# A gated recurrence and a top-2 router: TensorE's order written out by hand, one activation table, accumulating scatters, two weight buffers

## The chip, the cores and the metric

The kernel runs on one core of a Trainium2 chip. The metric is the device time of one execution in microseconds (us). The engines are TensorE (PE; its weight loads are listed as PEld), VectorE (DVE), ScalarE (ACT), GpSimd (POOL) and SyncE (SP), which here only issues DMAs.

## The reference

There are two parts, all in float32. The first is a gated recurrence for 4 batches of 8 heads, 768 steps, and a head size of 48; the second is a mixture of 8 experts over the 3072 rows of 384 numbers which the first part gives.

```python
f = 1 / (1 + exp(-f_logit))
for t in range(768):                              # per batch and head
    state = f[t][:, None] * state + outer(k[t], v[t])
    y[t] = q[t] @ state
x = y as rows: (batch, step) by (head, dim)       # 3072 x 384
noisy = x @ w_gate + log1p(exp(x @ w_noise)) * noise
top2 of 8 experts per row; their weights are a softmax over the two
out[row] = sum over its two experts e: weight * (relu(x[row] @ w1[e]) @ w2[e])
# w1[e] is 384 x 1024, w2[e] is 1024 x 384
```

## The kernel before

**Attention.** The steps are cut into 6 chunks of 128 per batch: 24 chunks, numbered n = c * 4 + b. All 8 heads of a chunk are one tile of 128 x 512 (each head padded to 64 columns). Five stages handle a chunk:

- `forget` (L480): POOL clamps f; PE transposes it; ACT makes exp, then ln(1 + .); POOL writes the first column of `cap` (L489); VectorE's scan adds up along the chunk (L490); ACT makes P = exp(-L) and Q = exp(L).
- `scaled` (L498): PE transposes q and k; VectorE multiplies them by P and Q (qP, kQ).
- `scores` (L504): PE multiplies kQ by qP; VectorE masks the result (A); PE transposes kQ back and ACT copies it (kn).
- `output` (L520): y is the sum of v by A (L526, 128 rows of the array) and of state by qP (L530, 64 rows), which alternate by pairs of heads; ACT copies it. Then ds = kn by v gives the next state of the batch (L539 to L549).
- `features` (L552): PE transposes y, ACT copies it and SP writes it to `x_rows` in DRAM; PE makes the router's logits (L563) in a PSUM bank that the four batches of a chunk share.

After each fourth chunk `route` (L567) makes the two experts of each of 512 rows, counts rows per expert with the matmuls L604 and L605 (`rk`), and POOL scatters one entry of 4 words for each row and expert into `lists` (L627): 8 indirect DMAs, 48 in all. An entry holds the row to read, the row of `out` to add (or a far one if this is the row's first expert), the weight, and the row of `out` to write.

**FFN.** `plan` (L634) forms 55 tiles of up to 128 rows, each of one expert, and writes to `steer` for each tile its expert, its place in the lists and whether its weights have to be loaded. For a tile, `fetch` (L671) has SP load the list entries and POOL gather the rows (L679); `weights` (L683) loads w1 and w2 (1.5 MB each) into one of NR = 3 buffers if `new` is set; `turned` (L688) transposes the rows; `hidden` (L696) makes 8 blocks of 128 hidden units with 48 matmul instructions, and ACT applies ReLU after each half (L704); `result` (L707) clears `had` and gathers the rows of `out` written so far into it (L710), multiplies by w2 (L715), scales and adds on VectorE (L718) and scatters to `out` (L720). `out` is zeroed at the start by 24 DMAs on POOL (L736).

**What sets the order.** The stages are written as a software pipeline (L741 to L749) and a loop over tiles (L764 to L772). A scheduler of the framework then orders the instructions of each engine by their place in the program and by modelled times of readiness, so an engine's order is not the written one. Each engine and each DMA queue works in its own order. PSUM has 4 single banks (`one_bank`) and 2 double ones (`two_banks`); a tile gets a bank when its last user is done. Dependencies of PSUM tiles are tracked by tile: in `hidden` the second half waits for ACT's read of the first.

Of the kernel before, what the change touches and what calls it, by code (L numbers as in the profile page):

```python
# [329 lines left out]
def kernel(  # L330
# [30 lines left out]

# [12 lines left out]
    NR = 3  # L374
# [24 lines left out]
    NLD = 4  # L399
    PAD = {"f": 30.0, "q": 0.0, "k": 0.0, "v": 0.0}  # L400
    pads = {n: [const.tile([C, H, DP], F32, tag=f"{n}{i}", name=f"{n}{i}") for i in range(NLD)] for n in "fqkv"}
    for i in range(NLD):
        for n in "fqkv":
            nc.vector.memset(pads[n][i][:, :, D:DP], PAD[n])

# [26 lines left out]
    for i, val in enumerate((0, FAR, 0, FAR)):  # L432
        nc.vector.memset(empty[:, :, i], val)
# [3 lines left out]
    for i in range(2):  # L437
        nc.gpsimd.memset(cap[i], LCAP)

# [27 lines left out]
    def load(n):  # L467
        c, b = n // B, n % B
        for nm, src in (("f", f_logit), ("q", q), ("k", k), ("v", v)):
            nc.sync.dma_start(out=pads[nm][n % NLD][:, :, 0:D],  # L470
                              in_=src[b, :, c * C:(c + 1) * C, :].rearrange("h t d -> t h d"))

    def transposed(nm, n):
        p = one_bank(f"{nm}p_{n}")
        flat = pads[nm][n % NLD].rearrange("t h d -> t (h d)")
        for hp in range(HP):
            nc.tensor.transpose(p[:, cols(hp)], flat[:, cols(hp)], ident)  # L477
        return p

    def forget(n):  # L480
        raw = pads["f"][n % NLD].rearrange("t h d -> t (h d)")
        nc.gpsimd.tensor_scalar(raw, raw, XMIN, None, ALU.max)  # L482
# [37 lines left out]
    def output(n):  # L520
        c, b = n // B, n % B
        vt = pads["v"][n % NLD]
# [29 lines left out]
    def features(n):  # L552
# [9 lines left out]
        for hp in range(HP):  # L562
            nc.tensor.matmul(lg[c][:, b, :], lhsT=yT[n][:, cols(hp)], rhs=w_rt[:, hp, :],  # L563
                             start=(hp == 0), stop=(hp == HP - 1))


    def route(c):  # L567
# [40 lines left out]
        late = t([B, 2], "late")  # L608
        nc.vector.tensor_tensor(late[:, :, 0:1], fx[:, :, 0:1], fx[:, :, 1:2], ALU.is_gt)
        nc.vector.tensor_tensor(late[:, :, 1:2], fx[:, :, 1:2], fx[:, :, 0:1], ALU.is_gt)  # L610
        entry = t([B, 2, 4], "entry", U32)
        tok = token[:, c, :].unsqueeze(2).broadcast_to((128, B, 2))
        prev = t([B, 2], "prev")
        nc.vector.tensor_scalar(prev, tok, -float(FAR), None, ALU.add)
        nc.vector.tensor_tensor(prev, prev, late, ALU.mult)
        nc.vector.tensor_scalar(entry[:, :, :, 1], prev, float(FAR), None, ALU.add)
        nc.vector.tensor_copy(entry[:, :, :, 0], tok)
        nc.vector.tensor_copy(entry[:, :, :, 3], tok)
        nc.vector.tensor_copy(entry[:, :, :, 2].bitcast(F32), ex)
# [5 lines left out]
        for b in range(B):  # L625
            for r in range(2):
                put = nc.gpsimd.indirect_dma_start(  # L627
                    out=lists, out_offset=bass.IndirectOffsetOnAxis(ap=sloti[:, r, b:b + 1], axis=0),
                    in_=entry[:, b, r, :], in_offset=None)
# [39 lines left out]
    w2 = [const.tile([128, FO, DM], F32, tag=f"w2_{i}", name=f"w2_{i}") for i in range(NR)]  # L669

    def fetch(t, steer):  # L671

        slots = ffn.tile([128, 4], U32, tag="slots", name=f"slots{t}", bufs=6)
        e, row, new = (nc.values_load(steer[0:1, t, i:i + 1], engines=[mybir.EngineType.SP], min_val=0, max_val=hi,
                                      skip_runtime_bounds_check_because="clamped where they are made")
                       for i, hi in ((0, E - 1), (1, E * N), (2, 1)))
        nc.sync.dma_start(out=slots, in_=lists[bass.ds(row, 128), :])
        xg = ffn.tile([128, DM], F32, tag="xg", name=f"xg{t}", bufs=4)
        nc.gpsimd.indirect_dma_start(out=xg, out_offset=None, in_=x_rows,  # L679
                                     in_offset=bass.IndirectOffsetOnAxis(ap=slots[:, 0:1], axis=0))  # L680
        return slots, xg, e, new

    def weights(t, e, new):  # L683
        i = t % NR
        nc.sync.dma_start(out=w1[i], in_=moe_w1[bass.ds(e, 1)].rearrange("o (k p) f -> p (o k) f", p=128), cond=new)
        nc.sync.dma_start(out=w2[i], in_=moe_w2[bass.ds(e, 1)].rearrange("o (f p) d -> p (o f) d", p=128), cond=new)

    def turned(t, xg):  # L688
        xp = one_bank(f"xgp{t}")
        for i in range(KO):  # L690
            nc.tensor.transpose(xp[:, i * 128:(i + 1) * 128], xg[:, i * 128:(i + 1) * 128], ident)  # L691
        xt = ffn.tile([128, KO, 128], F32, tag="xt", name=f"xt{t}")
        nc.vector.tensor_copy(xt, xp[:, 0:DM].rearrange("d (k t) -> d k t", k=KO))  # L693
        return xt

    def hidden(t, xt):  # L696
        hp = two_banks(f"hp{t}").rearrange("f a (o t) -> f a o t", t=128)
        hs = ffn.tile([128, FO, 128], F32, tag="hs", name=f"hs{t}")
        for fo in range(FO):
            for i in range(KO):  # L700
                nc.tensor.matmul(hp[:, fo // 4, fo % 4, :], lhsT=w1[t % NR][:, i, fo * 128:(fo + 1) * 128],  # L701
                                 rhs=xt[:, i, :], start=(i == 0), stop=(i == KO - 1))
# [4 lines left out]
    def result(t, hs, slots):  # L707
        had = ffn.tile([128, DM], F32, tag="had", name=f"had{t}")
        nc.gpsimd.memset(had, 0.0)  # L709
        nc.gpsimd.indirect_dma_start(out=had, out_offset=None, in_=out,  # L710
                                     in_offset=bass.IndirectOffsetOnAxis(ap=slots[:, 1:2], axis=0),
                                     bounds_check=N - 1, oob_is_err=False)
        yp = one_bank(f"yp{t}")
        for fo in range(FO):
# [3 lines left out]
        nc.vector.scalar_tensor_tensor(ys, in0=yp[:, 0:DM], scalar=slots[:, 2:3].bitcast(F32), in1=had,  # L718
                                       op0=ALU.mult, op1=ALU.add)
        nc.gpsimd.indirect_dma_start(out=out, out_offset=bass.IndirectOffsetOnAxis(ap=slots[:, 3:4], axis=0),  # L720
                                     in_=ys, in_offset=None, bounds_check=N - 1, oob_is_err=False)
# [17 lines left out]
    for n in range(NLD):  # L739
        load(n)  # L740
    for i in range(-2, NS + 2):  # L741
        for stage, lag in ((forget, -2), (scaled, -1), (scores, 0), (output, 1), (features, 2)):
            n = i - lag
            if 0 <= n < NS:
                stage(n)
                if stage is output and n + NLD < NS:
# [58 lines left out]
```

## Time and profile before

| what | value |
|---|---|
| median of 3 runs | 1020.29 us (1019.8 to 1022.79) |
| profiled execution | 1024.36 us, span 1022.6 us |
| mean granted clock of TensorE | 0.911 |
| PE busy | 859.0 us (84%) |
| weight loads busy | 673.4 us (66%) |
| VectorE, ACT, POOL busy | 194.5, 237.2, 312.3 us |
| DMA | 130.6 MB in 159,887 packets, mean 128 GB/s |

The span runs from the first to the last instruction. A share of busy time is a mean over two stages with different limits, so it says little by itself. The granted clock is the share of full speed (2.4 GHz) that TensorE got; 0.5 is its lower level, 1.2 GHz. Rows of matmuls have modelled ends and overlap, so starts are used for times between them. Where a row ends in square brackets, the engine sat idle before it for that many us, and the name is what ended this.

### The profile page before, as it was taken

The numbers are of one execution on the slowest core, as the hardware profiler recorded it, in microseconds if no ns is written. First come the engines' busy times: TensorE is split into PE (matmuls) and PEld (weight loads), VectorE is DVE, ScalarE is ACT, GpSimd is POOL, SyncE is SP. The second block draws the span as 40 slices with busy tenths as digits, with TensorE's granted clock in tenths as the row PEclk, the third lists the DMA queues.
The fourth block names the chain that finished last, engine by engine and source line by source line (L and its number), as shares of the span: only waits on it lengthen the run. The fifth ranks groups of instructions, "written<-read, shape, count | busy, mean of one in ns | idle before, by whom it ended". The sixth has DMA issues, their size and how long they took to land. (4 is left out here: it accounts for less than half of the span.)

```text
span 1022.6 us, 14847 instructions
## 1 busy us (share of the span) xinstructions
PE 859.0 (84%) x5777; PEld 673.4 (66%) x5777; DVE 194.5 (19%) x519; ACT 237.2 (23%) x357; POOL 312.3 (31%) x406
## 2 busy tenths in 40 slices
PE   0687979697891678899999899899899899999995
PEld 0575657475661556677777777677677677777773
DVE  1454434434503000000100010011010000011000
ACT  0785666565611000000101001001001001001010
POOL 7623343423033122232332333232223223233321
PEclk9898787887855889999999999899999999999998
DMA  9963525351100906616615713731841842941100
GB/s 297 116 121 72 102 59 100 66 106 33 39 24 17 383 25 217 217 42 214 230 37 165 268 51 109 248 119 49 284 159 49 283 165 63 315 138 55 47 18 4
DMA packets 159887, 130.60 MB, mean 128 GB/s; under 512 B 115045, under 2 KB 143353, under 8 KB 159808
## 3 DMA queue, kind: packets, MB, share of 16 engines
q1 hardware_dynamic: 145920, 99.61, 34.3%
q0 software_dynamic: 13888, 29.94, 9.3%
q8 instruction: 48, 0.79, 0.3%
q14 instruction: 31, 0.25, 0.1%
HBM read 213.75 MB, written 20.74 MB: 229 GB/s over the span
## 5 line engine op out<-in xcount | busy, mean ns | idle before, releaser
L701 PEld LDWEIGHTS hp<-xt,w 128*128 128x128 f32 x2640 | 315.6, 196 | 47.7 <-ACT hs L704 32.3
L701 PE MATMUL hp<-xt,w 128*128 128x128 f32 x2640 | 325.4, 281 | 22.5 <-ACT hs L704 21.8
L715 PE MATMUL yp<-w,hs 128*128 128x384 f32 x880 | 294.8, 489 | 0.0
L715 PEld LDWEIGHTS yp<-w,hs 128*128 128x128 f32 x880 | 164.2, 192 | 103.0 <-issue 1.8
L704 ACT ACTIVATE hs<-hp 128x512 f32<-128x512 f32 x110 | 65.7, 597 | 628.7 <-PE hp L701 613.3
L720 POOL DMA_INDIRECT out_dram<-ys,slots x55 | 55.2, 1004 | 290.0 <-DVE ys L718 289.7
L718 DVE SCALAR_TENSOR_TENSOR ys<-yp,slots,had 128x384 f32<-128x384 f32 x55 | 34.0, 618 | 439.6 <-PE yp L715 330.5
L710 POOL DMA_INDIRECT had<-out_dram,slots x55 | 56.6, 1030 | 179.1 <-issue 138.5
L691 PE MATMUL xgp<-ident,xg 128*128 128x128 f32 x165 | 29.3, 288 | 50.4 <-DMA xg<-x_rows,slots 50.3
L693 DVE COPY xt<-xgp 128x384 f32<-128x384 f32 x55 | 30.7, 558 | 187.3 <-PE xgp L691 181.5
L679 POOL DMA_INDIRECT xg<-x_rows,slots x55 | 53.0, 964 | 30.4 <-issue 14.3
L627 POOL DMA_INDIRECT lists<-entry,sloti x48 | 46.8, 975 | 32.2 <-DVE sloti L624 17.1
L691 PEld LDWEIGHTS xgp<-ident,xg 128*128 128x128 f32 x165 | 19.9, 146 | 53.2 <-issue 33.1
L526 PE MATMUL y<-A,v 128*64 128x128 f32 x384 | 47.5, 333 | 5.1 <-issue 4.8
L482 POOL TENSOR_SCALAR f<-f 128x512 f32<-128x512 f32 x24 | 36.6, 1527 | 31.4 <-DMA f<-in_f_logit_dram 31.3
L477 PE MATMUL fp<-ident,f 128*128 128x128 f32 x96 | 20.7, 355 | 29.2 <-POOL f L482 29.2
L530 PE MATMUL y<-qP,st 64*64 64x128 f32 x320 | 42.0, 343 | 1.7 <-issue 1.7
L490 DVE TENSOR_TENSOR_SCAN L<-f,cap 128x512 f32<-128x512 f32 x24 | 30.0, 1255 | 48.4 <-POOL cap L489 47.6
L526 PEld LDWEIGHTS y<-A,v 128*64 128x64 f32 x384 | 21.9, 153 | 23.0 <-issue 22.1
L477 PEld LDWEIGHTS fp<-ident,f 128*128 128x128 f32 x96 | 16.4, 205 | 29.6 <-POOL f L482 29.6
L530 PEld LDWEIGHTS y<-qP,st 64*64 64x64 f32 x320 | 18.6, 154 | 21.0 <-issue 21.0
L508 PE MATMUL sc<-qP,kQ 64*128 64x128 f32 x384 | 31.9, 312 | 0.0
(120 smaller groups left out, 621.1 us busy)
## 6 DMA issues: line engine op xcount, KB each, us to landing
w<-in_moe_w_dram SPq DMA_DIRECT2D x110, 1536.0 KB
f<-in_f_logit_dram SPq DMA_DIRECT2D x24, 192.0 KB
q<-in_q_dram SPq DMA_DIRECT2D x24, 192.0 KB
k<-in_k_dram SPq DMA_DIRECT2D x24, 192.0 KB
v<-in_v_dram SPq DMA_DIRECT2D x24, 192.0 KB
out_dram<-zero POOLq DMA_DIRECT2D x24, 192.0 KB
x_rows<-xs SPq DMA_DIRECT2D x24, 192.0 KB
slots<-lists SPq DMA_DIRECT2D x55, 2.0 KB
```

The source lines that it names most:

```text
L477: nc.tensor.transpose(p[:, cols(hp)], flat[:, cols(hp)], ident)
L482: nc.gpsimd.tensor_scalar(raw, raw, XMIN, None, ALU.max)
L526: nc.tensor.matmul(y[rows(par), cols(hp)], lhsT=vt[:, 2 * hp + par, :], rhs=A[n][:, par, cols(hp)], start=True, stop=(c == 0))
L530: nc.tensor.matmul(y[rows(par), cols(hp)], lhsT=state[b][rows(par), hp, :], rhs=qP[n][rows(par), cols(hp)], start=False, stop=True)
L627: put = nc.gpsimd.indirect_dma_start(out=lists, out_offset=bass.IndirectOffsetOnAxis(ap=sloti[:, r, b:b + 1], axis=0), in_=entry[:, b, r, ...
L679: nc.gpsimd.indirect_dma_start(out=xg, out_offset=None, in_=x_rows, in_offset=bass.IndirectOffsetOnAxis(ap=slots[:, 0:1], axis=0))
L691: nc.tensor.transpose(xp[:, i * 128:(i + 1) * 128], xg[:, i * 128:(i + 1) * 128], ident)
L701: nc.tensor.matmul(hp[:, fo // 4, fo % 4, :], lhsT=w1[t % NR][:, i, fo * 128:(fo + 1) * 128], rhs=xt[:, i, :], start=(i == 0), stop=(i == ...
L704: nc.scalar.activation(hs[:, fo - 3:fo + 1, :], hp[:, fo // 4], AF.Relu)
L710: nc.gpsimd.indirect_dma_start(out=had, out_offset=None, in_=out, in_offset=bass.IndirectOffsetOnAxis(ap=slots[:, 1:2], axis=0), bounds_ch ...
L715: nc.tensor.matmul(yp[:, 0:DM], lhsT=hs[:, fo, :], rhs=w2[t % NR][:, fo, :], start=(fo == 0), stop=(fo == FO - 1))
L720: nc.gpsimd.indirect_dma_start(out=out, out_offset=bass.IndirectOffsetOnAxis(ap=slots[:, 3:4], axis=0), in_=ys, in_offset=None, bounds_che ...
```

## The change

- **Order.** `in_order` adds to each TensorE instruction a scheduling edge from the one written before it, from the first load on. The other engines are ordered as before.
- **State matmuls.** In `output` all 8 pairs of v by A come first, then all of state by qP, with one start flag per bank.
- **Tables.** One set of ACT's tables, which has exp and ln, is loaded at the start.
- **Loads.** f, q and k have 3 buffers and v has 4. Each is refilled right behind the stage that last reads it, and the clamp of f moves from `forget` to the load.
- **Zeros.** The 24 writes of zeros to `out` move from POOL to SP, one behind each `output`.
- **Router.** The logits of a chunk get a bank of their own and are copied by ACT. `route` is cut in two: the part from `rk` on is written one iteration later. The row numbers of all entries are made at the start.
- **Scatters.** An entry holds the row, the weight, and the row of `out`. POOL's scatter adds to `out` in DRAM; `had`, its clearing and its gather go.
- **FFN.** NR is 2. List entries are loaded 4 tiles ahead and rows gathered 3 ahead, both written ahead of `hidden`; w1 of tile t + 2 is asked for behind `hidden(t)`, w2 behind `result(t)`. `turned(t + 1)` is written between `hidden(t)` and `result(t)`, as before.

```diff
-    NR = 3
+    NR = 2
...
-    NLD = 4
+    RING = {"f": 3, "q": 3, "k": 3, "v": 4}
...
+    nc.scalar.preload_act_table_set("natural_log_exp_and_others")
...
+    entry = const.tile([128, NCH, B, 2, 4], U32, tag="entry", name="entry")
+    nc.vector.memset(entry, 0)
+    for i in (0, 2):
+        nc.vector.tensor_copy(entry[:, :, :, :, i], token.unsqueeze(3).broadcast_to((128, NCH, B, 2)))
...
-    def load(n):
+    def load(nm, n):
         c, b = n // B, n % B
...
+        if n < NCH * B:
+            nc.sync.dma_start(out=pads[nm][n % RING[nm]][:, :, 0:D],
...
+            if nm == "f":
+                raw = pads["f"][n % RING["f"]].rearrange("t h d -> t (h d)")
+                nc.gpsimd.tensor_scalar(raw, raw, XMIN, None, ALU.max)
...
         for hp in range(HP):
             for par in range(2):
                 nc.tensor.matmul(y[rows(par), cols(hp)], lhsT=vt[:, 2 * hp + par, :], rhs=A[n][:, par, cols(hp)],
-                                 start=True, stop=(c == 0))
-            if c:
+                                 start=(hp == 0), stop=(c == 0 and hp == HP - 1))
+        if c:
+            for hp in range(HP):
                 for par in range(2):
                     nc.tensor.matmul(y[rows(par), cols(hp)], lhsT=state[b][rows(par), hp, :],
-                                     rhs=qP[n][rows(par), cols(hp)], start=False, stop=True)
+                                     rhs=qP[n][rows(par), cols(hp)], start=False, stop=(hp == HP - 1))
...
+        lp = one_bank(f"lp_{n}")[:, 0:2 * E]
+        for hp in range(HP):
+            nc.tensor.matmul(lp, lhsT=yT[n][:, cols(hp)], rhs=w_rt[:, hp, :],
+                             start=(hp == 0), stop=(hp == HP - 1))
         if b == 0:
-            lg[c] = one_bank(f"lg_{c}")[:, 0:B * 2 * E].rearrange("t (b e) -> t b e", b=B)
...
+            lg[c] = rt.tile([128, B, 2 * E], F32, tag="lg", name=f"lg_{c}")
+        nc.scalar.copy(lg[c][:, b, :], lp)
...
+        yield
         rk = one_bank(f"rk_{c}")[:, 0:B * E].rearrange("t (b e) -> t b e", b=B)
...
-        late = t([B, 2], "late")
...
+        nc.vector.tensor_copy(entry[:, c, :, :, 1].bitcast(F32), ex)
...
-    def result(t, hs, slots):
-        had = ffn.tile([128, DM], F32, tag="had", name=f"had{t}")
-        nc.gpsimd.memset(had, 0.0)
-        nc.gpsimd.indirect_dma_start(out=had, out_offset=None, in_=out,
...
+        nc.vector.tensor_scalar(ys, yp[:, 0:DM], slots[t][:, 1:2].bitcast(F32), None, ALU.mult)
+        nc.gpsimd.indirect_dma_start(out=out, out_offset=bass.IndirectOffsetOnAxis(ap=slots[t][:, 2:3], axis=0),
+                                     in_=ys, in_offset=None, bounds_check=N - 1, oob_is_err=False, compute_op=ALU.add)
+    def in_order(first):
+        pe = [i for i in nc.cur_bb.bb.instructions[first:] if i.engine == mybir.EngineType.PE]
+        for a, b in zip(pe, pe[1:]):
+            tc.add_manual_dep(b, a.name, mybir.DependencyInfo(mybir.DependencyClass.NoSync, mybir.DependencyReason.DATA),
+                              reason="order of TensorE")
...
-    for i in range(0, N, 128):
-        nc.gpsimd.dma_start(out=out[i:i + 128, :], in_=zero)
...
     for i in range(-2, NS + 2):
         for stage, lag in ((forget, -2), (scaled, -1), (scores, 0), (output, 1), (features, 2)):
             n = i - lag
...
+            stage(n)
+            if stage is forget:
+                load("f", n + 3)
+            elif stage is scaled:
+                load("q", n + 3)
+                load("k", n + 3)
+            elif stage is output:
+                load("v", n + 4)
+                nc.sync.dma_start(out=out[n * 128:(n + 1) * 128, :], in_=zero)
+        for r in routing:
+            next(r, None)
+        routing = []
+        if i >= 2 and (i - 2) % B == B - 1:
+            routing = [route((i - 2) // B)]
+            next(routing[0])
...
+    AHEAD = 4
     for t in range(AHEAD):
+        fetch(t)
+    for t in range(NR):
+        weights(t, 1)
+        weights(t, 2)
+    for t in range(AHEAD - 1):
+        gather(t)
+    turned(0)
     for t in range(NB):
         if t + AHEAD < NB:
+            fetch(t + AHEAD)
+        if t + AHEAD - 1 < NB:
+            gather(t + AHEAD - 1)
+        hs = hidden(t)
+        if t + NR < NB:
+            weights(t + NR, 1)
         if t + 1 < NB:
+            turned(t + 1)
+        result(t, hs)
+        if t + NR < NB:
+            weights(t + NR, 2)
+    in_order(first)
```

## Rows read from the trace of the kernel before

**Rows 1.** Windows by stage: length, busy (instructions) per engine, clock, DMA share, GB/s.

```profile
0.00:28.82 28.82, 0.00 (x0) 0.00 (x1) 3.85 (x27) 1.28 (x1) 23.27 (x51) 1.00 1.10 281
28.82:40.23 11.41, 6.69 (x29) 5.56 (x29) 4.39 (x5) 7.70 (x12) 8.84 (x9) 0.92 1.24 130
40.23:308.60 268.37, 226.93 (x2057) 174.17 (x2056) 112.94 (x322) 159.16 (x230) 83.82 (x119) 0.79 0.37 73
308.60:328.39 19.79, 1.70 (x8) 1.54 (x8) 8.69 (x56) 3.43 (x6) 8.95 (x11) 0.50 0.03 9
328.39:339.04 10.65, 0.88 (x4) 0.51 (x4) 0.56 (x1) 0.00 (x0) 2.03 (x2) 0.50 0.80 268
339.04:1011.64 672.60, 622.75 (x3682) 491.60 (x3682) 63.48 (x109) 65.67 (x110) 184.39 (x214) 0.98 0.44 146
```

**Rows 2.** Waits, PE's own: us in total, times, longest.

```profile
PE xgp L691 <- DMA xg<-x_rows,slots: 50.3, 15, 22.4
...
PE rk L604 <- DVE late L610: 28.4, 6, 4.8
...
PE hp L701 <- ACT hs L704: 21.8, 45, 0.7
```

**Rows 3.** Timeline of POOL at the start: start, length, instruction.

```profile
21.56 1.19 POOL L447 DMA_DIRECT2D w_rt<-in_moe_w_gate_dram  x2 [0.38 <-issue]
...
27.27 5.87 POOL L482 TENSOR_SCALAR f<-f 128x512 f32<-128x512 f32 x4
```

**Rows 4.** Groups by line, whole kernel: busy, mean ns of one, idle before and releaser.

```profile
L627 POOL DMA_INDIRECT lists<-entry,sloti x48 | 46.8, 975 | 32.2 <-DVE sloti L624 17.1 <-issue 12.8 <-DVE kQ L502 2.3
...
L485 ACT ACT_TABLE_LOAD x23 | 29.5, 1283 | 0.4
...
L576 ACT ACT_TABLE_LOAD x6 | 7.7, 1283 | 0.1
```

**Rows 5.** Groups by line of the weight loads, 122.67 to 130.83.

```profile
L526 PEld LDWEIGHTS y<-A,v 128*64 128x64 f32 x16 | 0.8, 134 | 0.7 <-issue 0.7
L530 PEld LDWEIGHTS y<-qP,st 64*64 64x64 f32 x16 | 0.8, 131 | 0.7 <-issue 0.7
L539 PEld LDWEIGHTS ds<-v,kn 128*64 128x64 f32 x16 | 0.5, 137 | 0.2 <-DVE A L511 0.2
...
L516 PEld LDWEIGHTS kp<-ident,kQ 128*128 128x128 f32 x4 | 0.4, 140 | 0.1
```

**Rows 6.** Windows around the route of the second chunk group.

```profile
132.00:137.00 5.00, 0.30 (x2) 0.33 (x3) 3.89 (x32) 2.42 (x4) 0.00 (x0) 0.71 0.02 7
137.00:142.00 5.00, 5.00 (x32) 4.28 (x31) 2.83 (x14) 3.40 (x5) 0.19 (x1) 0.61 0.48 94
...
148.00:152.00 4.00, 1.96 (x20) 1.36 (x20) 0.22 (x1) 1.72 (x2) 2.92 (x4) 0.89 0.41 81
152.00:165.00 13.00, 12.40 (x80) 8.95 (x82) 5.16 (x7) 7.13 (x11) 5.44 (x7) 0.51 0.48 83
```

**Rows 7.** Window of the first weight loads.

```profile
334.00:356.00 22.00, 16.02 (x90) 13.15 (x91) 1.74 (x3) 1.19 (x2) 2.03 (x3) 0.81 1.05 386
```

**Rows 8.** Timeline of one late FFN tile.

```profile
930.72 2.84 PE L701 MATMUL hp<-xt,w 128*128 128x128 f32 x24
...
931.81 1.00 POOL L720 DMA_INDIRECT out_dram<-ys,slots  x1 [5.85 <-DVE ys L718]
...
933.28 0.36 PEld L691 LDWEIGHTS xgp<-ident,xg 128*128 128x128 f32 x3
...
933.65 0.60 ACT L704 ACTIVATE hs<-hp 128x512 f32<-128x512 f32 x1 [7.30 <-PE hp L701]
...
934.30 2.94 PE L701 MATMUL hp<-xt,w 128*128 128x128 f32 x24 [0.42 <-ACT hs L704]
935.18 1.03 POOL L710 DMA_INDIRECT had<-out_dram,slots  x1 [1.94 <-issue]
...
942.25 2.84 PE L701 MATMUL hp<-xt,w 128*128 128x128 f32 x24
```

More of the change, by code (lines that the diff above doesn't have):

```diff
@@ L431 @@
     empty = const.tile([128, LR // 128, 4], U32, tag="empty", name="empty")
-    for i, val in enumerate((0, FAR, 0, FAR)):
+    for i, val in enumerate((0, 0, FAR, 0)):
         nc.vector.memset(empty[:, :, i], val)
@@ L521, in output @@
         c, b = n // B, n % B
[L522 removed]
+        vt = pads["v"][n % RING["v"]]
         y = one_bank(f"y_{n}")
@@ L669 @@
     w2 = [const.tile([128, FO, DM], F32, tag=f"w2_{i}", name=f"w2_{i}") for i in range(NR)]
[L671 to L688, printed above, removed]
+    slots, xg, xt, reg = {}, {}, {}, {}
+    def fetch(t):
+        slots[t] = ffn.tile([128, 4], U32, tag="slots", name=f"slots{t}", bufs=8)
+        row = nc.values_load(steer[0:1, t, 1:2], engines=[mybir.EngineType.SP], min_val=0, max_val=E * N,
+                             skip_runtime_bounds_check_because="clamped where it is made")
+        nc.sync.dma_start(out=slots[t], in_=lists[bass.ds(row, 128), :])
@@ new lines, in gather, with weights @@
+    def gather(t):
+        xg[t] = ffn.tile([128, DM], F32, tag="xg", name=f"xg{t}", bufs=4)
+        nc.gpsimd.indirect_dma_start(out=xg[t], out_offset=None, in_=x_rows,
+                                     in_offset=bass.IndirectOffsetOnAxis(ap=slots[t][:, 0:1], axis=0))
+    def weights(t, which):
+        if which == 1:
+            reg[t] = [nc.values_load(steer[0:1, t, i:i + 1], engines=[mybir.EngineType.SP], min_val=0, max_val=hi,
+                                     skip_runtime_bounds_check_because="clamped where they are made")
+                      for i, hi in ((0, E - 1), (2, 1))]
+        e, new = reg[t]
+        if which == 1:
+            nc.sync.dma_start(out=w1[t % NR], in_=moe_w1[bass.ds(e, 1)].rearrange("o (k p) f -> p (o k) f", p=128), cond=new)
+        else:
+            nc.sync.dma_start(out=w2[t % NR], in_=moe_w2[bass.ds(e, 1)].rearrange("o (f p) d -> p (o f) d", p=128), cond=new)
@@ L689, in turned @@
+    def turned(t):
         xp = one_bank(f"xgp{t}")
         for i in range(KO):
[L691 to L696, printed above, removed]
+            nc.tensor.transpose(xp[:, i * 128:(i + 1) * 128], xg[t][:, i * 128:(i + 1) * 128], ident)
+        xt[t] = ffn.tile([128, KO, 128], F32, tag="xt", name=f"xt{t}")
+        nc.vector.tensor_copy(xt[t], xp[:, 0:DM].rearrange("d (k t) -> d k t", k=KO))
@@ L697, in hidden @@
+    def hidden(t):
         hp = two_banks(f"hp{t}").rearrange("f a (o t) -> f a o t", t=128)
@@ L734 @@
     nc.vector.memset(zero, 0.0)
-    for i in range(0, N, 128):
-        nc.gpsimd.dma_start(out=out[i:i + 128, :], in_=zero)
     load_router()
     NS = NCH * B
-    for n in range(NLD):
-        load(n)
+    first = len(nc.cur_bb.bb.instructions)
+    for i in range(3):
+        for nm in "fqkv":
+            load(nm, i)
+    load("v", 3)
+    routing = []
     for i in range(-2, NS + 2):
@@ L743 @@
             n = i - lag
-            if 0 <= n < NS:
-                stage(n)
-                if stage is output and n + NLD < NS:
-                    load(n + NLD)
-                if stage is features and n % B == B - 1:
-                    route(n // B)
+            if not 0 <= n < NS:
+                continue
+            stage(n)
[9 more added lines that the diff above has]
+            next(r, None)
+        routing = []
+        if i >= 2 and (i - 2) % B == B - 1:
+            routing = [route((i - 2) // B)]
+            next(routing[0])
+    for r in routing:
+        next(r, None)
     beyond()
```

52 lines of the change are left out of this document (8 added, 44 removed).

## The prediction

> **What bounds the kernel now.** I read the busy time by stage first, then the waits of TensorE (PE), then single stretches. [rows 1] splits the span of 1022.6 us: PE does nothing for 28.8 us, fills the pipeline for 11.4, runs the attention for 268.4, waits 19.8 for the last route and its scatters and 10.7 for the first gather, works 672.6 us in the feed-forward stage (FFN), and 11.0 are left behind it. PE is busy for 622.8 of the 672.6 us (clock 0.98) and for 226.9 of the 268.4 us, but there the granted clock is 0.79. So PE bounds both stages: the FFN by its work, the attention by its work, its clock and 41.4 us of idleness. In [rows 2] the reader is to see what ends PE's idle times: late gathers (50.3 us, of which 22.4 are the start of the FFN), the rank matmuls behind VectorE (28.4 us, 6 times), and the second half of a tile behind the ReLU of its first half (21.8 us, 45 times).
>
> **The start.** [rows 3]: POOL issues 24 zero writes first, then the router loads, and comes to the clamp of f at 27.27; PE's first transposes follow at 28.82. The change moves the zero writes to SP, one behind each chunk. POOL's router loads (21.56 to 27.27: 5.7 us) then stand first, from about 4 us, and the first transposes come at about 11 us: -17.8. Bounds: 6.5 (clamp ahead of the router loads) and 16 (loads late, since SP issues them in a burst). The zero writes now fall into the attention: 24 x 192 KB = 4.7 MB. Its DMA share is 0.37 [rows 1] and would be about 0.55 in the shorter stage, so they hide; if that cover is gone, 4.7 MB at the 281 GB/s of the first stretch is 17 us. SP's queue gets 24 more issues, none of which waits (the zeros are made at the start).
>
> **Load rings.** f, q and k go from 4 buffers to 3, but each is refilled right behind the stage that frees it, two or three chunks ahead of its use. A chunk's transfers take 0.37 x 268.4 / 24 = 4.1 us of the DMA engines [rows 1], under a chunk of 7 us: I cost it at nothing. If a chunk came later than that, PE would wait at the transposes; POOL's clamp now stands right behind the load, ahead of later work on POOL, so a late f would hold that too.
>
> **Activation tables.** ACT loads a table 58 times: two per chunk (23 each at L485 and L493) and two per route (6 each at L576 and L587), 1,283 ns each [rows 4]. Preloading one set that holds exp and ln takes 74 us off ACT. But ACT's 159 us in 268 [rows 1] are not the bound; on the path stand only two loads in the fill (11.4 to about 9: -2.4) and two in the last route (-2.6). The Trainium skill ("ScalarE: Activation LUTs", What ACT_TABLE_LOAD costs) charges 1.28 us for the load and 1.38 more for a drain. The trace disagrees: before the 23 loads at L485 ACT is idle for 0.4 us in all [rows 4], so no drain of that size shows. By the page the two places would give 10 us in place of 5.
>
> **The attention: gaps inside a chunk.** [rows 5] is one chunk at full clock, from its first transposes (122.67) to the next scores (130.83): 8.16 us. Its y matmuls change between values (K=128, L526) and state (K=64, L530) 8 times, and the weight loads of the two lines sit idle 0.7 us each: 0.17 us a change. Grouped apart, 2 changes stay: 6 x 0.17 = 1.0, so 7.1 us. The first four chunks have no state matmuls (0.8 + 0.2 less), the last four neither ds nor key transposes (0.7 + 0.5 less): 16 x 7.1 + 4 x 6.1 + 4 x 5.9 = 162 us, 3 of them before the first scores: 159. ACT is left with about 90 us of work (159 less some 54 table loads), VectorE 113, POOL 84 [rows 1], all below PE. In the written order each matmul uses tiles that other engines made an iteration earlier, so PE should wait for PSUM banks at most.
>
> **The attention: waits and clock.** [rows 6] follows one route. 132 to 137: the rank matmuls stand in PE's queue ahead of VectorE's work for them; PE is busy for 0.3 of 5 us, and in the next 5 us the clock is 0.61, mostly its 1.2 GHz level, although PE is busy throughout. 148 to 152: eight list scatters hold POOL (0.975 us each and 0.30 between them [rows 4]: 10 us in all); PE is busy for 2.0 of 4 us, and the next 13 us run at 0.51. Five routes show the pair. The change moves the second half of a route one iteration later (7 us); VectorE's part of it is 3.9 us of busy time (first row of [rows 6]), so I take the 28.4 us and the first kind of fall as gone. The scatters stay, 48 with the same pitch and in a burst, and I keep the second kind: 41.4 - 28.4 = 13 us of idleness, and 5 falls of some 10 us at half speed, 5 us lost in each: 25. Attention: 159 + 13 + 25 = 197 us. Bounds: 167 (bursts absorbed) and 248 (only the 1.0 us a chunk won). The extra copy of the logits (24 on ACT) lies beside PE and frees the bank that a group's logits held; a wait for it stops the next key transposes.
>
> **Last route to the first hidden matmul.** From 19.79 us the two tables (2.6) and seven small VectorE operations for `late`, `prev` and `entry` (0.5) go, a copy comes (0.2): 16.8. Then 10.65 [rows 1]: four list fetches now precede the first weights on SP, some 2 us, but the weights are 6 MB where 9 MB ran at 386 GB/s with the DMA engines full [rows 7], so the first gather lands sooner. I take 10.5, between 6 and 14.
>
> **The FFN tile.** [rows 8]: the first 24 hidden matmuls start at 930.72 and end at 933.56; the next tile's transposes load from 933.28; ReLU ends at 934.25 and the second half starts at 934.30, 3.58 us behind the first. The next tile starts at 942.25: 11.53 us a tile. The second half waits for that ReLU in any order, since `hidden` stays as it is. In the written order the transposes come behind the second half; they no longer lie in the gap and cost 0.36 us: 11.89. 54 x 11.89 + 11.47 = 653.6, and 2.5 for a first tile at half clock: 656. Against it go the late gathers behind the start: 50.3 - 22.4 = 27.9 us, with falls of the clock behind them. They were late because POOL's gather stood behind the read of `had`, which waits for the scatter before it to land (issued 931.81, read issued 935.18), and behind 9 MB of weights. Now a gather is asked for three tiles ahead, its list four, and `had` is gone. So 672.6 becomes 656: between 637 (the transposes cost nothing) and 684 (all 27.9 us stay).
>
> **Two weight buffers.** The buffer of tile t is refilled behind tile t - 2: the first weights are asked for 17 us, the second 19 us before use, and 1.5 MB at 386 GB/s take 4.1 us [rows 7]: nothing on the path. Without that cover a new expert would cost up to 8 us, 7 times.
>
> **Accumulating scatters.** No row shows one. A plain scatter landed within 3.4 us [rows 8], and the read that it replaces fitted into a tile of 11.5, so both together take 3.4 to 15 us; I take 7, twice the nearest row. The Trainium skill ("DMA: Bandwidth & Descriptors", Rules for kernel authors) says that an accumulating DMA has to wait for the semaphore of an earlier one on the same bytes; no row here shows that wait. At 7 us in a tile of 11.9 a wait of each scatter for the one before adds nothing; queued behind it on POOL are the gathers, which have two tiles to spare. At the end it adds 0 to 4 us to the 11.0; I take 11.
>
> **Sum.** 11 + 9 + 197 + 16.8 + 10.5 + 656 + 11 = 911.3 us against 1022.6: -111.3. The profiled execution took 1024.36 us (1.8 around its span), 4.1 above the median of 1020.29, from which I subtract: 909 us.
>
> **Rivals.** (a) *The bursts are absorbed* and the clock stays at 2.4 GHz: no PE operand comes from the scatters directly. Against it: five of five bursts stopped PE. Attention 167, and 4 us for a quicker gather: 875. (b) *A new wait takes the old one's place*: a strict order can't fill a hole with other matmuls, four single banks serve eight tiles a chunk, and one late VectorE step stops all. Against it: VectorE and ACT are half idle. Attention 248: 960. (c) *The table loads stay*: ACT has 159 + 5 us in 197, close to PE, with 5 us more in fill and route and about 10 of waits: 924. (d) *Slower: the scatters chain.* Reads of `out` already wait for its writes [rows 8], so a scatter may wait for the one before. If it takes longer than a tile, the FFN runs at 55 times its pace. All else wins 95 us, so this decides from (656 + 111) / 55 = 14 us; at the bound of 15 the FFN is 825 us and the kernel takes 1078. For it: nothing shows the price. Against: the separate read and write together fitted in 11.53 us.
>
> **Chances.** Forecast (885 to 940) 0.52, (a) 0.17, (b) 0.14, (c) 0.11 (inside the forecast's range), (d) 0.06. Faster 0.92, same 0.02 (the far end of (b)), slower 0.06, with 0.3% (3 us) as what a measurement can tell. The range 870 to 960 leaves out the far ends of (a) and (b) and all of (d).
>
> **What would show it.** Right: first transposes near 11 us; one table load; y in two blocks of 16 with one change each; the rank wait gone; clock falls only at the list scatters; FFN tiles 11.9 us apart with PE idle 0.7 us ahead of each second half; no wait for a gather but the first. Wrong: tiles 11.5 us or less apart, PE idle before scores or y in every chunk, ACT still loading tables, or a scatter on POOL that waits for the one before.

## The result, and the profile after

The changed kernel takes 920.95 us (median of 4 runs, 920.59 to 922.33) against 1021.54 (1019.8 to 1024.09) on the same chip: ratio 0.9016, interval 0.8992 to 0.904. The forecast was 909, its range 870 to 960. The profiled execution spans 918.8 us.

The windows by stage of the changed kernel [rows 1] (length; busy time and instructions of PE, PEld, DVE, ACT, POOL; clock; DMA share; GB/s):

```profile
0.00:11.10 11.10, 0.00 (x1) 0.00 (x1) 3.53 (x23) 1.28 (x1) 10.37 (x27) 1.00 1.06 158
11.10:22.80 11.70, 6.94 (x28) 5.41 (x28) 4.13 (x5) 5.24 (x9) 3.66 (x7) 1.00 1.48 154
22.80:222.85 200.05, 172.43 (x2057) 149.13 (x2056) 112.19 (x288) 90.99 (x198) 86.74 (x121) 0.93 0.64 127
222.85:241.95 19.10, 1.80 (x9) 1.59 (x8) 8.66 (x52) 1.07 (x5) 9.62 (x10) 0.54 0.05 13
241.95:253.74 11.79, 0.88 (x3) 0.53 (x4) 0.56 (x1) 0.00 (x0) 3.86 (x4) 0.50 0.63 217
253.74:908.16 654.42, 613.44 (x3682) 486.03 (x3682) 63.49 (x108) 65.67 (x110) 135.40 (x105) 1.00 0.40 105
```

The start became 17.7 us shorter, the attention 68.3, the FFN 18.2; in the attention the clock rose from 0.79 to 0.93 and ACT has 68 us less work. The waits of the changed kernel [rows 2] (us in total, times, longest), PE's and two of others:

```profile
PE hp L708 <- ACT hs L711: 41.0, 55, 0.7
PE qp L485 <- DVE mid L556: 23.8, 4, 6.1
PE xgp L699 <- issue: 19.6, 1, 19.6
...
PE hp L708 <- DMA w<-in_moe_w_dram: 4.8, 1, 4.8
PE rk L615 <- DVE sm L600: 3.7, 1, 3.7
PE rk L616 <- DVE before L612: 1.7, 4, 0.4
```

```profile
POOL out_dram L721 <- DVE ys L720: 434.9, 55, 19.7
...
DVE L L496 <- POOL cap L495: 46.8, 9, 13.3
```

The rank matmuls waited 28.4 us, 4.8 of them in the last route; now it is 1.7, and 3.7 in the last route. Only one gather still stops PE, the first. In their place stands one wait in four places, `PE qp <- DVE mid`, and the ReLU wait now stands in all 55 tiles. What holds DVE there is seen on the timeline of one burst of list scatters (start, length, instruction, idle before and releaser):

```profile
147.48 0.96 POOL L627 DMA_INDIRECT lists<-entry,sloti  x1 [0.30 <-issue]
148.74 0.96 POOL L627 DMA_INDIRECT lists<-entry,sloti  x1 [0.30 <-issue]
...
148.97 0.63 PE L485 MATMUL fp<-ident,f 128*128 128x128 f32 x4
...
152.53 0.95 POOL L627 DMA_INDIRECT lists<-entry,sloti  x1 [0.30 <-issue]
153.48 0.21 POOL L495 COPY cap<-f 128x4 f32<-128x4 f32 x1
153.72 1.63 DVE L496 TENSOR_TENSOR_SCAN L<-f,cap 128x512 f32<-128x512 f32 x1 [7.96 <-POOL cap L495]
155.27 0.39 DVE L556 TENSOR_TENSOR mid<-ds,st 128x256 f32<-128x256 f32 x1
155.72 1.11 PE L485 MATMUL qp<-ident,q 128*128 128x128 f32 x4 [6.12 <-DVE mid L556]
```

A 0.2 us copy on POOL stands behind eight scatters, the scan waits for the copy, `mid` stands behind the scan in DVE's queue, and PE's next transposes wait for `mid`, which reads the PSUM bank of `ds` that they take over. Afterwards PE runs at its lower level, as the windows over this burst show [rows 6]:

```profile
150.00:155.00 5.00, 0.00 (x0) 0.00 (x0) 1.28 (x1) 0.00 (x0) 4.39 (x5) 0.78 0.37 60
155.00:160.00 5.00, 4.16 (x25) 3.31 (x26) 3.18 (x6) 2.71 (x6) 1.15 (x4) 0.53 0.36 89
```

The weight loads of one chunk at full clock, 133.75 to 140.89 [rows 5] (count, busy, mean ns, idle before): the y loads sit idle 0.2 us each where they had 0.7.

```profile
L533 PEld LDWEIGHTS y<-A,v 128*64 128x64 f32 x16 | 0.9, 136 | 0.2 <-issue 0.2
L538 PEld LDWEIGHTS y<-qP,st 64*64 64x64 f32 x16 | 0.8, 132 | 0.2 <-issue 0.2
```

One FFN tile on the timeline [rows 8]:

```profile
410.20 2.84 PE L708 MATMUL hp<-xt,w 128*128 128x128 f32 x24
...
411.30 1.62 POOL L721 DMA_INDIRECT out_dram<-ys,slots  x1 [3.28 <-DVE ys L720]
...
413.79 2.94 PE L708 MATMUL hp<-xt,w 128*128 128x128 f32 x24 [0.75 <-ACT hs L711]
416.46 0.36 PEld L699 LDWEIGHTS xgp<-ident,xg 128*128 128x128 f32 x3
...
422.06 2.84 PE L708 MATMUL hp<-xt,w 128*128 128x128 f32 x24
```

11.86 us from tile to tile: PE stands 0.75 us ahead of the second half, and the next tile's transposes come behind it.

### The profile page after: what moved, and what is told of

Same layout as the page of the kernel before. It is cut to its first block, busy times and chain, and to the rows that moved or that the text cites. A ratio compares the mean times of both kernels' runs of the same rounds, so it can differ in the third digit from the quotient of the medians.

```text
span 918.8 us, 14545 instructions
## 1 busy us (share of the span) xinstructions
PE 795.5 (87%) x5777; PEld 642.7 (70%) x5777; DVE 193.2 (21%) x477; ACT 164.3 (18%) x323; POOL 251.2 (27%) x272
## 4 chain that ended last, share of the span: by engine, by line
PE 67%; ACT 4%; DMA 1%; issue 1%; POOL 1%; SPq 0%; ACTq 0%; DVE 0%; POOLq 0%
PE hp L708 34%; PE yp L717 31%; ACT hs L711 4%; PE xgp L699 2%; DMA w<-in_moe_w_dram 1%; POOL lists L627 1%; DMA lists<-entry,sloti 0%; SPq L677 0%; POOL out_dram L721 0%; ACTq L711 0%; SPq L675 0%; DVE ys L720 0%; SPq L687 0%; POOLq L801 0%; SPq L692 0%
## 5 line engine op out<-in xcount | busy, mean ns | idle before, releaser
L708 PE MATMUL hp<-xt,w 128*128 128x128 f32 x2640 | 320.6, 278 | 45.8 <-ACT hs L711 41.0
L708 PEld LDWEIGHTS hp<-xt,w 128*128 128x128 f32 x2640 | 309.8, 193 | 71.0 <-ACT hs L711 51.5
L721 POOL DMA_INDIRECT out_dram<-ys,slots x55 | 86.9, 1579 | 434.9 <-DVE ys L720 434.9
L720 DVE TENSOR_SCALAR ys<-yp,slots 128x384 f32<-128x384 f32 x55 | 34.0, 618 | 259.6 <-PE yp L717 259.6
L627 POOL DMA_INDIRECT lists<-entry,sloti x48 | 46.8, 976 | 32.4 <-DVE sloti L624 19.6
L699 PE MATMUL xgp<-ident,xg 128*128 128x128 f32 x165 | 27.4, 275 | 19.6 <-issue 19.6
L485 PE MATMUL qp<-ident,q 128*128 128x128 f32 x96 | 17.5, 313 | 24.9 <-DVE mid L556 23.8
L479 POOL TENSOR_SCALAR f<-f 128x512 f32<-128x512 f32 x24 | 35.7, 1488 | 11.2 <-DMA f<-in_f_logit_dram 10.6
L485 PEld LDWEIGHTS qp<-ident,q 128*128 128x128 f32 x96 | 13.1, 162 | 26.1 <-DVE mid L556 24.7
L514 PEld LDWEIGHTS sc<-qP,kQ 64*128 64x128 f32 x384 | 27.3, 216 | 4.7 <-issue 4.7
L517 DVE TENSOR_TENSOR A<-sc,causal 128x1024 f32<-128x1024 f32 x24 | 29.1, 1211 | 1.0 <-PE sc L514 0.5
L499 ACT ACTIVATE P<-L 128x512 f32<-128x512 f32 x24 | 15.1, 631 | 67.3 <-DVE L L496 67.3
L533 PE MATMUL y<-A,v 128*64 128x128 f32 x384 | 26.3, 279 | 0.0
```

Source lines behind the costliest of these rows:

```text
L514: nc.tensor.matmul(sc[:, par, cols(hp)], lhsT=kQ[n][rows(par), cols(hp)], rhs=qP[n][rows(par), cols(hp)], start=True, stop=True)
L627: put = nc.gpsimd.indirect_dma_start(out=lists, out_offset=bass.IndirectOffsetOnAxis(ap=sloti[:, r, b:b + 1], axis=0), in_=entry[:, c, b, ...
L699: nc.tensor.transpose(xp[:, i * 128:(i + 1) * 128], xg[t][:, i * 128:(i + 1) * 128], ident)
L720: nc.vector.tensor_scalar(ys, yp[:, 0:DM], slots[t][:, 1:2].bitcast(F32), None, ALU.mult)
```

## The experiments

They ran on three chips, on which the kernel before took 1028 to 1033 us (medians), where it took 1021.54 beside the first result. The changed kernel was run again on one of them; differences are taken from that run, stages from the profiles. On the two others the base is inferred: kernels there whose attention is that of the changed kernel (plain last scatter, two one-bank tiles) or differs from it in TensorE's order alone start their last rank matmul at 234.3 to 235.7 us, the changed kernel run again at 235.24. Times that an expectation gives in us were mostly counted from the first result's 921, so it is the differences that are compared.

**The changed kernel again.**

> The changed kernel once more, unaltered, beside the two kernels that follow. Theory: the attention of one and the same code comes out differently from run to run (in the changed kernel's profile the last rank matmul L615 starts at 226.6 us, in the kernels with a plain last scatter and with two hidden banks, whose attention is the same code, at 235.7 and 234.3), because the fifth burst of scatters sometimes stops the last two chunks and sometimes not: here the last rank matmul starts at 234 to 236 us and the time is 928 to 932 us. Rival: something in those two kernels' later part delayed their attention: here 226 to 228 us and 919 to 923 us.

928.92 us (927.15 to 929.36), ratio 0.9, 0.8939 to 0.9061; the last rank matmul starts at 235.24 us, where the first profile had 226.60. The theory holds for the place: everything from that matmul to the end takes 692 us in both. That it changes from run to run is not shown: the four times of the first result lie within 1.8 us of each other, the four here within 2.3. Of the 8.6 us, 7.2 lie behind the last chunk's `qP`: from its start to the last rank matmul it takes 18.7 us in the first profile and 25.9 here. There the fifth burst runs, and in the first profile PE is busy throughout the first six of its eight scatters (7.80 of 7.80 us from 215.05 on), while here gaps stand between its matmuls, as in the burst of which the first profile's timeline is above. That one looks like this here, PE's rows and one window:

```profile
150.45 0.49 PE L564 MATMUL xp<-ident,yT 128*128 128x128 f32 x3 [0.82 <-issue]
150.78 0.18 PE L570 MATMUL lp<-w_rt,yT 128*128 128x16 f32 x1
151.18 0.18 PE L570 MATMUL lp<-w_rt,yT 128*128 128x16 f32 x1 [0.22 <-issue]
151.89 0.62 PE L570 MATMUL lp<-w_rt,yT 128*128 128x16 f32 x4 [0.53 <-issue]
153.32 0.29 PE L570 MATMUL lp<-w_rt,yT 128*128 128x16 f32 x2 [0.82 <-issue]
155.47 1.09 PE L485 MATMUL fp<-ident,f 128*128 128x128 f32 x4 [1.86 <-POOL cap L495]
```

```profile
150.00:155.00 5.00, 1.59 (x11) 1.41 (x10) 0.09 (x1) 0.22 (x1) 4.09 (x6) 0.93 0.03 2
```

The scatters run from 144.72 to 154.68. In their second half PE's matmuls come singly, with 0.2 to 0.8 us between them for which the profile names no releaser, and the DMA engines are almost idle. So a burst can also slow engines that wait for nothing on POOL; what carries that, and why the fifth burst of the first profile did not, the profiles don't show.

**Order not fixed.**

```diff
-    in_order(first)
```

> The changed kernel without the written order of TensorE (the scheduler orders it again); all else as changed. My theory: the order is what keeps the rank matmuls from standing ahead of VectorE's work, and it costs the FFN 0.27 us a tile (11.80 against 11.53). So the rank waits come back in the attention (5 x 4.7 us idle and some 6 us lost to the clock: +45 to +50) and the FFN wins 15: about 950 us. Rival: the split of the route alone keeps the rank matmuls late, the scheduler's order is as good in the attention, and only the FFN changes: about 906 us.

912.64 us (911.79 to 914.65), ratio 0.8848, 0.8786 to 0.8911: my theory was wrong, the rival right. The last rank matmul stands at 235.13 us, as with the fixed order (235.24), and the gain is all in the FFN: the planner itself puts the next tile's transposes between the two halves.

```profile
414.55 2.84 PE L708 MATMUL hp<-xt,w 128*128 128x128 f32 x24
...
417.23 0.49 PE L699 MATMUL xgp<-ident,xg 128*128 128x128 f32 x3
...
418.14 2.94 PE L708 MATMUL hp<-xt,w 128*128 128x128 f32 x24 [0.42 <-ACT hs L711]
```

The tile is back at 11.53 us (403.02 to 414.55), as before the change: 0.33 x 54 = 17.8, measured 16.3.

**Table loads back.**

```diff
-    nc.scalar.preload_act_table_set("natural_log_exp_and_others")
```

> The changed kernel without the preloaded activation table. My theory: ACT is not the bound (91 of 200 us busy in the attention; 159 with the tables), so only the loads in the fill and the last route count, and a few us of later ReLU-like copies behind the clock falls: +5 to +12, 926 to 933 us. Rival: ACT's chain (exp, table, ln, scan, table, exp) decides each chunk once PE is faster: +25 or more.

954.06 us (952.67 to 955.08), ratio 0.9239, 0.9175 to 0.9304: 25 us slower than the changed kernel, against my 5 to 12; the rival was right. ACT on the timeline:

```profile
51.01 0.60 ACT L489 ACTIVATE f<-fp 128x512 f32<-128x512 f32 x1 [0.37 <-PE fp L484]
51.62 1.28 ACT L490 ACT_TABLE_LOAD   x1
52.92 0.63 ACT L490 ACTIVATE f<-f 128x512 f32<-128x512 f32 x1
53.57 1.28 ACT L498 ACT_TABLE_LOAD   x1
55.55 0.63 ACT L498 ACTIVATE P<-L 128x512 f32<-128x512 f32 x1 [0.70 <-DVE L L495]
...
58.87 0.60 ACT L489 ACTIVATE f<-fp 128x512 f32<-128x512 f32 x1 [0.37 <-PE fp L484]
```

With two loads ACT's round (exp, load, ln, scan on VectorE, load, exp, copies) takes 7.4 to 7.9 us, of which it is idle for about 1. The starts of `qP` show where that costs: in the first group, which has no state matmuls, it comes 7.6 to 8.3 us apart after the fill, where it came 5.5 to 6.6 apart (6.8 us in all); a chunk away from a route takes 7.42 in place of 7.08; and the chunk with the first half of a route, which adds to ACT's work, 9.5 to 10.4 in place of 8.1 to 8.3. In the kernel before, a chunk took PE 8.2 us from the second group on, longer than this round; in the first group `qP` already came 7.7 to 7.9 us apart.

**y not grouped.**

```diff
-                                 start=(hp == 0), stop=(c == 0 and hp == HP - 1))
-        if c:
-            for hp in range(HP):
+                                 start=True, stop=(c == 0))
+            if c:
...
```

> The changed kernel with the value and state matmuls alternating again. My theory: six more changes between 128 and 64 rows a chunk, 0.17 us each, on PE's path in 20 chunks: +20 us at full clock, some more at half: 941 to 947 us. Rival: PE waits in each chunk for something else, and the gaps lie in that wait: within 5 us of 921.

939.58 us (938.35 to 940.83), ratio 0.91, 0.9036 to 0.9163: 10.7 slower, half of my 20 and twice the rival's 5. Its y loads again sit idle 0.7 us each in a chunk. Away from a route `qP` comes 7.98 us after the last one in place of 7.08, so the 0.9 us a chunk is nearly as forecast. But the chunk with the first half of a route gets only 0.2 to 0.3 us longer and the one that a burst stops 0 to 0.7, so 12 us of the 20 show at the last rank matmul (247.2 us): the rest lies in waits that were there anyway.

**Zero writes at the start, on POOL.**

```diff
+    for i in range(0, N, 128):
+        nc.gpsimd.dma_start(out=out[i:i + 128, :], in_=zero)
...
-                nc.sync.dma_start(out=out[n * 128:(n + 1) * 128, :], in_=zero)
```

> The changed kernel with the 24 zero writes back on POOL ahead of the router loads. My theory: the first transposes move from 11 back to about 28 us, and the attention gets almost nothing for it: +14 to +18, 935 to 939 us. Rival: the zeros' 4.7 MB hold up loads in the attention (DMA share 0.64 there), and what is lost at the start is partly won back: +8 or less.

940.78 us (940.35 to 941.83), ratio 0.9117, 0.9054 to 0.918: 11.9 slower, between the rival's 8 and my 14 to 18. The first transposes come at 28.41 us in place of 11.10, but the first scores 7.5 us behind them in place of 11.7, because by then the loads of f have landed: 17.3 - 4.2 = 13.1.

**Route in one piece.**

```diff
-        yield
         rk = one_bank(f"rk_{c}")[:, 0:B * E].rearrange("t (b e) -> t b e", b=B)
...
                 tc.add_to_no_dep_group("lists", put.ins)
+        yield
```

> The changed kernel with the route in one piece: the rank matmuls are written right behind its first half. My theory: PE now waits at the rank matmuls for the whole of VectorE's work, about 5 us in each of 5 routes, and the clock falls behind it: +35 to +60 us, 955 to 980. Rival: PE waits at the list scatters anyway, a little later, and the two waits overlap: +15 or less.

951.34 us (949.92 to 952.38), ratio 0.9239, 0.9204 to 0.9274: 22.4 slower, between the rival's 15 and my 35 to 60. Its waits show the rank matmuls again: `rk <- DVE sm` 22.5 us, 6 times (the changed kernel: 3.7, once); that the wait and the stop by the scatters partly overlap, as the rival had it, fits but is not shown.

**Plain last scatter.**

```diff
-                                     bounds_check=N - 1, oob_is_err=False, compute_op=ALU.add)
+                                     bounds_check=N - 1, oob_is_err=False)
```

> The changed kernel with a plain scatter in place of the accumulating one (so out holds only the later of a row's two experts). My theory: the accumulation is hidden behind a tile of 11.8 us; POOL's instruction gets shorter (1.58 to about 1.0 us) and the end at most 2 us earlier: 918 to 921 us. Rival: the accumulating DMA takes DMA time or order that others wait for: 5 us or more won.

930.65 us (929.78 to 932.84), ratio 0.9036, 0.9003 to 0.9069: no gain. From the first hidden matmul (263.31 us) to the last `ys` (917.44) it takes 654.1 us, the changed kernel 654.3 (262.37 to 916.65). An accumulating scatter holds POOL for 1.58 us, a plain one for 1.01. The accumulating one lands 4.4 us behind its issue (median; 2.7 to 8.2). None of it is on the path. The Trainium skill ("DMA: Bandwidth & Descriptors", Rules for kernel authors) tells the kernel to have an accumulate wait for the semaphore of an earlier one on the same bytes. With a scatter each 11.86 us that landed within 8.2 no such wait could show, and the only releaser of POOL's scatters is `ys`, 55 times.

**The copy cap on ScalarE.**

```diff
-        nc.gpsimd.tensor_copy(top[:, :, 0], f.rearrange("d (a t) -> d a t", t=C)[:, :, 0])
+        nc.scalar.copy(top[:, :, 0], f.rearrange("d (a t) -> d a t", t=C)[:, :, 0])
```

> The changed kernel with the 4-column copy into cap on ACT in place of POOL. My theory: a burst of eight list scatters stops PE only because this copy stands behind it in POOL's queue, so the scan waits, and VectorE's next step (mid) waits behind the scan. With the copy on ACT the 4 stops of 5.9 us and the falls of the clock behind them (3 to 3.5 us each) go, and the fill wins 2: 880 to 887 us. Rival: the burst slows the others in another way (their signals, the DMA queues, the shared port): 10 us or less won.

917.87 us (917.52 to 918.74), ratio 0.8914, 0.8881 to 0.8946: 11 won where I expected some 40; the rival's 10 was near. Of the 11, 4.4 are won at the start (the first `qP` at 16.7 in place of 21.1 us), 6.7 in the bursts. The scan no longer waits, but in the burst PE and DVE still stand:

```profile
142.43 0.63 PE L485 MATMUL fp<-ident,f 128*128 128x128 f32 x4
...
145.87 0.42 DVE L556 TENSOR_TENSOR mid<-ds,st 128x256 f32<-128x256 f32 x1 [5.76 <-remote]
146.35 1.12 PE L485 MATMUL qp<-ident,q 128*128 128x128 f32 x4 [3.29 <-issue]
```

**Two scatters a chunk.** `route` yields behind each pair, and each pair is ordered behind the last POOL instruction written before it.

```diff
         for b in range(B):
+            late = [i for i in nc.cur_bb.bb.instructions if i.engine == mybir.EngineType.Pool][-1]
             for r in range(2):
...
+                tc.add_manual_dep(put.ins, late.name, mybir.DependencyInfo(mybir.DependencyClass.NoSync, mybir.DependencyReason.DATA),
+                                  reason="two scatters a chunk")
+            yield
...
```

> Two of the eight list scatters a chunk over four chunks instead of eight in a row, all else as changed. Theory: eight scatters in a row on POOL delay every other engine's signals and instructions (PE stands 6 us, then runs at half clock for about 2 us' worth), 4 bursts of 8.3 us each beyond four chunks at 7.14 us, the fifth 0 to 9 us; two at a time delay nothing: bursts at 37.9 us apart become 29 to 30, and the time falls by 32 to 42 us, to 882 to 900. Rival A: the delay belongs to each scatter, wherever it stands: no gain, 915 to 932. Rival B: only the small copy cap, the first POOL instruction behind the eight, matters: the gain is that of cap on ScalarE, about 11 us, 908 to 920.

906.41 us (904.85 to 908.53), ratio 0.8781, 0.8721 to 0.8841: 22.5 won, under the theory's 32, twice rival B's 11, and rival A is out. Two scatters beside a chunk cost it nothing (qP of neighbouring chunks 7.08 us apart, 142.50 and 149.58). The fifth burst is not spread: its eight scatters still run in a row at 196 to 206 us, and 25.9 us pass from the last `qP` to the last rank matmul, as before. Three chunks with the first half of a route still take 9.4 to 12.1 us, where the changed kernel took 8.1 to 8.3. In the longest of them cap stands behind the second scatter of a fourth chunk, the scan starts 2.4 us late, and the route's VectorE work stands behind it:

```profile
124.26 0.97 POOL L628 DMA_INDIRECT lists<-entry,sloti  x1 [0.30 <-issue]
...
125.23 0.20 POOL L495 COPY cap<-f 128x4 f32<-128x4 f32 x1
...
128.40 1.07 PE L570 MATMUL lp<-w_rt,yT 128*128 128x16 f32 x8 [1.46 <-ACT kn L524]
```

**Two one-bank tiles for the hidden halves.**

```diff
-        hp = two_banks(f"hp{t}").rearrange("f a (o t) -> f a o t", t=128)
+        hp = [one_bank(f"hp{t}_{a}").rearrange("f (o t) -> f o t", t=128) for a in range(2)]
...
```

The transposes `xgp` and the result `yp` change places with them and go to the double banks.

> The changed kernel with the two halves of the hidden matmuls in two PSUM tiles of one bank, and the transposes and the result in the double ones. My theory: PE's wait for ReLU between the halves (0.70 to 0.75 us, 55 times) comes only from tracking both halves as one tile, and goes: a tile takes 11.1 us, 880 to 885 us in all. Rival: another wait takes its place (the turned rows, a bank of the result): 15 us or less won.

873.22 us (872.1 to 875.06), ratio 0.8477, 0.8446 to 0.8509: 55.7 won, more than I expected. All 48 hidden matmuls run through, and PE is hardly idle in the stage (596.6 of 597.0 us busy from 263 to 860); a tile takes 10.85 us, and 55 x 1.01 = 55.6:

```profile
407.36 5.52 PE L708 MATMUL hp<-xt,w 128*128 128x128 f32 x48
...
418.21 5.52 PE L708 MATMUL hp<-xt,w 128*128 128x128 f32 x48
```

So the second half never needed the ReLU of the first: it writes another bank, and waited because both halves were one tile.

**The same, order not fixed.** The edit of the two banks and that of the free order together.

> Hidden halves in two one-bank tiles, and TensorE's order not fixed by hand. Theory: without the fixed order the planner had put the next tile's transposes between the hidden halves, into the wait for ReLU, and won 0.32 us a tile (11.53 against 11.85 us); where that wait is gone already (tile 10.85 us) nothing is left to win: 870 to 877 us, the tile 10.8 to 10.9 us. Rival: the written order itself costs the 17 us of the second half: 854 to 860 us, the tile 10.5 us.

873.73 us (873.01 to 875.01), ratio 0.8472, 0.8414 to 0.8529: nothing more, as the theory had it. The free order wins only by filling the ReLU gap.

**All together.** Two banks, cap on ScalarE and two scatters a chunk as above, and the first weights ahead of the list fetches:

```diff
-    for t in range(AHEAD):
+    fetch(0)
+    weights(0, 1)
+    weights(0, 2)
+    for t in range(1, AHEAD):
         fetch(t)
-    for t in range(NR):
-        weights(t, 1)
-        weights(t, 2)
+    weights(1, 1)
+    weights(1, 2)
```

> Four edits on the changed kernel together: two one-bank tiles for the hidden halves, cap copied on ScalarE, two list scatters a chunk instead of eight in a row, and the first tile's two weight transfers issued ahead of the list fetches of tiles 1 to 3. Theory: they add up, because they work in different places. The second half takes 10.85 us a tile, 639 us from the last rank matmul to the end as with the two banks alone; the last rank matmul, at 214.7 us with the scatters spread alone, comes 3 us earlier by the earlier start and some 8 us earlier because cap no longer stands behind the two scatters of a fourth chunk (two stops of about 4 us are left in the spread kernel, at 125 and 159 us): 203 to 207 us; the first hidden matmul's wait for its weights falls by 0 to 4 us: 839 to 847 us in all. Rival: cap and the spread scatters remove the same stops, and only the two-bank and the spread gains add: 848 to 856 us. Rival B: with the stops gone the loads or the route's own chain on VectorE become the limit in the attention, and half of the spread gain is lost: 857 to 865 us.

833.56 us (831.5 to 836.28), ratio 0.8119, 0.8085 to 0.8152: faster than both kernels and than the theory. The windows by stage (fill, attention, to the first hidden matmul, FFN); the first scores come at 20.67 us here:

```profile
11.10:20.67 9.57, 6.34 (x28) 5.33 (x28) 4.19 (x5) 6.38 (x13) 3.15 (x4) 0.88 1.46 152
20.67:187.20 166.53, 162.71 (x2057) 142.59 (x2056) 108.66 (x288) 94.11 (x218) 89.52 (x99) 1.00 0.81 155
187.20:218.89 31.69, 2.68 (x12) 2.12 (x12) 9.24 (x53) 1.07 (x5) 10.73 (x11) 0.53 0.31 111
218.89:820.00 601.11, 598.82 (x3682) 481.70 (x3682) 64.11 (x109) 65.67 (x110) 138.53 (x108) 1.00 0.42 113
```

PE is busy for 162.7 of 166.5 us at full clock. The last rank matmul comes at 190.96 us, 44.3 earlier than in the changed kernel run again; cap alone gave 11.0 and the spreading alone 20.5, so some 12.7 are left over. Of these, 7.2 lie behind the last `qP` (18.7 us to the last rank matmul in place of 25.9): the fifth burst, still eight in a row, lets PE run on (busy for 7.80 of 7.80 us from 179.40 on). So it did in the first profile of the changed kernel without any of these edits, so these 7.2 us can't be put down to them. For the other 5.5 a reason is at hand, which no run separates: each edit alone leaves the other's stop standing, and the lower clock behind it. The early weights won nothing: from the last rank matmul to the first hidden one it takes 27.9 us (27.1 in the changed kernel), now for the first gather.

## Why the prediction was right

By the terms of its sum, forecast and profiled: start 11 and 11.1; fill 9 and 11.7; attention 197 and 200.05; last route 16.8 and 19.1; to the first hidden matmul 10.5 and 11.8; FFN 656 and 654.4; tail 11 and 10.6. The span is 7.5 us over the 911.3; the near hit is in part luck, since in the profile of the run again the attention took 208.7. The other 4.5 us of the miss of 12 are the step from the profiled execution to the median: I took off 2.3, and here 2.15 are to be added.

- **Start and zero writes**: right. The fill was mis-sized: the first scan waited 13.3 us for cap, which stood on POOL behind a clamp that waited for its load of f. I had taken only the table loads off it; an earlier start meets loads that haven't landed.
- **Table loads** (5 us): the step that failed. I priced them by the kernel before, in which PE's longer chunk hid them from the second group on; beside a chunk of 7.1 us they would have cost 25. The sum did not suffer from that, because the attention was added up from PE's work. Rival (c) named the mechanism and gave 15. The Trainium skill ("ScalarE: Activation LUTs", What ACT_TABLE_LOAD costs) adds 1.38 us of drain to a load; the trace doesn't agree: with the loads back ACT is again idle for 0.4 us in all before 23 of them.
- **Gaps inside a chunk** (8.16 to 7.1): right; 7.14 us measured.
- **Rank wait and the split route** (28.4 us and the first falls gone): right in kind; undone, it costs 22.4. That the written order had a part in it fell with the order experiment.
- **Last route** (16.8; 19.1): mis-sized. Only the first of its two table loads lay on the path. The second ran in the kernel before from 310.61 to 311.89 us, beside VectorE's search for the two experts, for which ACT had to wait until 312.45.
- **Bursts kept** (13 us idle, 25 by the clock): the sum was right for the first profile, the shares were not. The 13 were 41.4 less all 28.4 us of rank waits, but 4.8 of these lie in the last route, outside the 268.4: 17.8 would have been left. The combined kernel's 162.7 us at full clock come near the 159 of work. In the first profile 27.6 us are idle and, measured against that, some 10 lost by the clock (172.4 less 162.7); in the second 26.1 and some 20. I had not said what the bursts stop: it is the copy behind them on POOL, and in some bursts PE and VectorE themselves, by a way that stays open.
- **FFN tile** (11.89): right, 11.86; no gather but the first is waited for. **Two weight buffers** and **accumulating scatters**: right in costing nothing; the scatter lands in 4.4 us, not 7.
- **First weights**: of the 11.8 us PE waits 4.8 for them, asked for behind four list fetches; moving them ahead turned it into a wait for the gather.

Rival (a), 875 us with the bursts absorbed, was not what happened, but its attention of 167 us was to be had, as the 166.5 of the combined kernel show. (b) came small, as the 23.8 us of `PE qp <- DVE mid`; (d) didn't occur.

Not every part of the change was undone by itself. The load rings, the second weight buffer and the gathers asked for earlier were not; that the late gathers went shows in PE's waits alone, 50.3 us before and 19.6 after, all of it now the first.

## What to carry to other kernels

Price an operation that is now hidden against the chunk that the change will leave, not against the one that hides it today. Before you write an engine's order by hand, look at what the planner had put into each gap, and look first whether the gap has to be there: two halves in one PSUM tile wait for each other, in two they don't. Spread a burst of indirect scatters over the pipeline, and put nothing small that others wait for behind it.

## What the hardware showed

- Eight list scatters in a row (0.96 us each, 0.30 between) can slow engines that wait for nothing on POOL: in one burst PE's matmuls came with gaps of 0.2 to 0.8 us, and the DMA engines moved 2 GB/s in 5 us. In another, the fifth of the first profile, PE was busy for 7.80 of 7.80 us. Two in a row beside a chunk did not lengthen it.
- The same kernel's attention took 200.05 us in one profile and 208.7 in the other; 7.2 of the difference lie behind the last `qP`, where the fifth burst stopped PE in one and not in the other.
- An accumulating scatter of 128 rows holds POOL 0.57 us longer than a plain one (1.58 against 1.01 us).
